# RWKV-7 with a hard-swish FFN on one core: turns of b and k from TensorE to VectorE, copies of y to GpSimd, scan ends to ScalarE

## The chip, the cores and the metric

The kernel runs on one core of one Trainium2 chip. The time is the device time of one execution in microseconds. Before the change three runs took 773.76, 773.98 and 776.44 us, median 773.98 us.

## What is computed

An attention block of the RWKV-7 kind feeds an FFN. For each of 4 batches and 8 heads (head dimension 40) a 40x40 state goes through 768 time steps:

```python
y[:, :, t] = np.einsum('bhd,bhde->bhe', rt, state)
Sa = np.einsum('bhde,bhe->bhd', state, at)
state_decay = state * wt[:, :, None, :] - np.einsum('bhd,bhe->bhde', Sa, bt)
state = state_decay + np.einsum('bhd,bhe->bhde', vt, kt)
```

y, as 3072 tokens of 320 features, is x of the FFN: `h = x @ w_in` (2048 wide), `g = h * clip(h + 3, 0, 6) / 6`, `out = g @ w_out`. The two weights come as 64-bit floats and are made into 32-bit ones on the chip.

## The kernel before

**Units.** The recurrence is computed in blocks of 64 time steps. A unit is one such block of a pair of batches: 128 partitions hold two batches of 64 steps, or, once turned, two heads of 64 (40 used) features. There are 24 units, i = 0 to 23; four make a group. For every unit `prepare(i)` (L582) makes what does not depend on the state, and `step(i)` (L883) what does:

- W, gam: w is turned by TensorE (L506), ScalarE writes it into `wm` (L595, L599), two scans on VectorE (L603, L614) give the cumulative products. gamma (`gam`) and its inverse (`rgam`) are put together from the ends of both scans: two copies of the second scan's result (L626 on ScalarE for the first four units, L628 on VectorE after them) and two by GpSimd (L632, L633).
- A, B, K: a, b and k turned so that features are on the partitions, times gamma or its inverse (L650, L658, L736). From unit 8 on a is not turned by TensorE: it is loaded "by quarters" (L478: 32 partitions for 32 time-step pairs, so that a transpose of 32x32 blocks on VectorE, L528, does the turn). b is turned by TensorE in eight halves (L516) from unit 8 on, k in four whole turns (L506); both products read PSUM.
- F, E, factor, EV: products of these (L672 or L685, L554, L752), the inverse's turn (L705) and K and B times the inverse on GpSimd (L725), which read the untransposed b and k.
- R, C, S, U, UT, rS, H, ysn in `step`: products with the state; ysn (L1064) gives y and the new state. r is loaded by quarters too and turned by VectorE (L531).
- move, move2: y goes into `xt`, the FFN's input, with features on the partitions: four DMAs for the first 256 features (L1111) and four of 32 partitions for the last 64 (L1116). `xt` has six rotating buffers, shared with two partial sums.

For each group the matrix 1 - F of all its units is inverted on VectorE in a chain of some 60 small operations with transposes at both ends (`invert`, L784 to L818), fed in between other work.

**FFN.** `expand` (L1171, L1184, L1193, L1194) and `contract` (L1219) work in pieces of four matmuls, handed out one by one between the attention's stages (`pieces`). An expand needs the two buffers of h, which are free once VectorE has made gt of the one before (L1194).

**Order.** The order of all instructions on each engine is that of the program text. From unit 4 on `a_block(m)` emits step m; a unit takes four steps. Stages of the unit at hand and of units ahead are emitted together: products first, in the order of PRODUCTS (L1463), then the rest in the order of RESULTS (L1465). Unit u >= 8 begins to be prepared at step max(3(u - 8), 4(u - 9)): 0, 3, 6, 9, 12, 16, 20 and so on; so the first four follow one another in three steps, the rest in four.

**Queues.** Nearly all DMAs are issued by SyncE, in program order; a load waits in that queue until its buffer is free, and what is behind it waits too. A unit has 2 loads of w, 4 of a, 2 of b, 2 of k, 8 of r, 4 of v, 8 moves and 2 stores of the output.

**Weights.** 20 pieces; pieces of the first 256 features are loaded by two DMAs, of 80 and 48 partitions (FEATURES, L259).

Of the kernel before, what the change touches and what calls it, by code (L numbers as in the profile page):

```python
# [17 lines left out]
P = 128  # L18
BL = 64
# [12 lines left out]
def kernel(  # L32
# [179 lines left out]
    area = const.tile([P, EDGE + 3 * H * BL], F32, name="area")  # L212
# [30 lines left out]
    tinv = const.tile([P, NH, BL], F32, name="tinv")  # L243


    state, last_dec = [], []
    for p in range(NP):
# [12 lines left out]
        [(0, 0, 2 * D), (2 * D, 4 * D, D + 8)],  # L260
        [(0, 2 * D, 2 * D), (2 * D, 6 * D, D + 8)],
        [(0, 5 * D + 8, L), (L, 7 * D + 8, L)],
# [188 lines left out]
    def fetch(name, i, engine=None):  # L451

        if i is None or i >= NK:
            return
        x, crossed = {"W": (w, 0), "A": (a, 0), "B": (b, 0), "K": (k, 0), "R": (r, 1),
                      "V": (v, 1)}[name]
        if name == "V":
            t = values[i % AHEAD]
        else:
            t = placed.get((name, i))  # L460
            if (name, i) == ("R", 1):
                t = others["K"]
            if (name, i) == ("W", NU + 1):
                t = values[NU]
            t = t if t is not None else (others if i < 2 * NU and i % 2 and name != "R" else inputs)[name]
        g, p = names[i]
        engines = engine or nc.sync
        if name == "R" and i >= NU or name == "A" and i >= 2 * NU:
            y = x[2 * p:2 * p + 2, :, g * BL:(g + 1) * BL, :]
            n = 2 if name == "R" else 1  # L470
            y = y.rearrange("q (k s j) t e -> s j (q k) (t e)", s=2, j=n).rearrange(
                "s j k (l e) -> s j l k e", e=2 * D)
            for s in range(2):
                for c in range(0, D, L):
                    z = s * SLOT + c
                    to = rooms[name][z:z + L].rearrange("l (j k e) -> l j k e", j=n, e=2 * D)
                    for j in range(n):
                        nc.sync.dma_start(out=to[:, j, :, 0:2 * D - c], in_=y[s, j, :, :, c:])  # L478
            data[i][name + "N"] = t
            return  # L480
# [43 lines left out]
    def turn_blocks(to, name):  # L524

        x = rooms[name].rearrange("p (j k y e) -> p j k y e", j=2, y=2, e=D)[:, :, :, :, 0:L]
        if name == "A":
            nc.vector.transpose(out=to[:].rearrange("p r (q t y) -> p q r y t", q=2, y=2), in_=x)  # L528
            return
# [32 lines left out]
    def begun_beside():  # L562

        begin = -(-(SCAN + 1) // 16) * 16
        for n, name in enumerate("KB"):
            x = area[:, begin + n * H * JOIN:begin + (n + 1) * H * JOIN]
            nc.gpsimd.memset(x, 0.0)
            beside[name] = x.rearrange("p (h t) -> p h t", h=H)
        beside["E"] = grp.tile([P, H, BL], F32, name="E", tag="U", bufs=1)
        nc.gpsimd.memset(beside["E"][:], 0.0)  # L570
        for name in "rgam", "RT":
            beside[name] = tmp.tile([P, NPR, P], F32, name=name, tag="rgam", bufs=2)
# [9 lines left out]
    def prepare(i, F):  # L582
        n, o = i % NU, data[i]
        halves = i >= 2 * NU
# [23 lines left out]
        def gam_stage():  # L608
# [15 lines left out]
            def copy(to, x):  # L624
                if i < NU:
                    nc.scalar.activation(out=to, in_=x, func=AF.Copy)  # L626
                else:
                    nc.vector.tensor_scalar(to, x, 1.0, None, ALU.mult)  # L628

            copy(gv[:, :, 0:HB], _ap(o["wm"], HB + 1, [[row, NB], [-1, HB]]))  # L630
            copy(rv[:, :, HB:BL], _ap(o["wm"], HB + 3, [[row, NB], [1, HB]]))
# [6 lines left out]
            if NU + 1 < i <= 2 * NU:  # L638
                fetch("V", i)
            yield from ()  # L640
# [12 lines left out]
        def b_stage():  # L653
            x = turn_in(o["BN"], halves)
            yield PE
            bt = o["bt"] = turned("bt")
            for y, z, g in zip(parts_of(bt, halves), x, parts_of(o["rg"], halves)):
# [74 lines left out]
        def k_stage():  # L732
            x = turn_pairs(o["KN"])
            yield PE
            kt = o["kt"] = turned("kt")
            nc.vector.tensor_tensor(out=kt[:], in0=x[:], in1=o["rg"][:], op=ALU.mult)  # L736
# [24 lines left out]
        return {"W": w_stage, "gam": gam_stage, "A": a_stage, "B": b_stage, "F": f_by_32 if i < 2 * NU else f_by_64,  # L761
# [121 lines left out]
    def step(i):  # L883
# [216 lines left out]
        def s_move():  # L1100
            xt = m["xt"] = ffn.tile([P, 3, P], F32, name="xt", bufs=6)
            yg = m["yg"]
            moves = m["moves"] = [(xt[0:D, 0:2], yg[0:D, 0:2, :]),
                     (xt[D:2 * D, 0:2], yg[SLOT:SLOT + D, 0:2, :]),
                     (xt[2 * D:3 * D, 0:2], yg[0:D, 2:4, :]),
                     (xt[3 * D:P, 0:2], yg[SLOT:SLOT + 8, 2:4, :])]
            for c in range(4):
                moves.append((xt[c * L:(c + 1) * L, 2],
                              yg[SLOT + 8:SLOT + D, 2 + c % 2, :]))
            for dst, src in moves[:4]:  # L1110
# [3 lines left out]
        def s_move2():  # L1114
            for dst, src in m["moves"][4:]:
                nc.sync.dma_start(out=dst, in_=src)  # L1116
# [94 lines left out]
    def contract(i, r, gts):  # L1211
# [13 lines left out]
        if r == 0:  # L1225
            sums[i] = op
            if split:
                part = ffn.tile([P, 3 * P], F32, name="part", tag="xt", bufs=6)[:, 0:DM]
# [219 lines left out]
    for _ in range(18):  # L1448
# [10 lines left out]
    AHEAD_STAGES = [["W", "gam"], ["A", "B"], ["F", "K"], ["E", "factor"], ["EV"]]  # L1459
    CLOSE_STAGES = [["W", "gam"], ["A", "B"], ["F", "K", "factor"], ["E"], ["EV"]]  # L1460
# [4 lines left out]
    RESULTS = ["ysn", "W", "VT", "EV", "R", "S", "C", "A", "B", "move", "move2", "open",  # L1465
               "U", "UT", "rS", "F", "K", "fade", "H", "E", "factor", "RT", "gam"]
# [42 lines left out]
    def a_block(m):  # L1509

        if coming and begins[coming[0]] == m:
            u = coming.popleft()
            close = coming and begins[coming[0]] < m + BLOCKS
            ahead[u, m] = prepared(u), CLOSE_STAGES if close else AHEAD_STAGES
# [29 lines left out]
    for i in range(NU, NK):  # L1544
        spread[0] = i >= 2 * NU - 1
        for j in range(BLOCKS):
# [20 lines left out]
            m += 1  # L1567
    for _ in range(2):
# [36 lines left out]
```

## Time and profile before

| | |
|---|---|
| runs | 773.76, 773.98, 776.44 us |
| profiled execution, its own time | 772.7 us |
| its span | 771.0 us |
| mean granted TensorE clock | 0.956 |
| DMA | 48.43 MB in 175999 packets, 159216 of them under 512 B |
| DMA share in the span's 40 slices, first to eighth | 9, 6, 8, 5, 5, 6, 3, 4 tenths |
| TensorE busy, 300 to 760 us | 20.00 of every 20 us |
| VectorE busy, 500 to 520 us (an inversion) | 18.80 of 20 us |
| VectorE busy, 540 to 560 us | 9.14 of 20 us |

Rows of groups read: line, engine, operation, written tile <- read tiles, shapes and count | busy time in us, mean ns of one | idle time of the engine just before them, and what ended it. In the chain and in timelines each row is a start and a length in us, then what ran; SPq is SyncE's queue, whose length is the time that it took to issue the DMAs (a wait that a DMA instruction itself holds is part of it).

### The profile page before, as it was taken

What the parts mean: (1) busy time and instruction counts of PE and PEld (TensorE: products, weight loads), DVE (VectorE), ACT (ScalarE), POOL (GpSimd) and SP (SyncE); (2) the same over time, 40 slices, a digit from 0 to 9 for tenths busy, and PEclk for the clock granted to TensorE, in tenths of its full rate; (3) what the DMA queues carried; (4) which work ended last, traced back from release to release, by engine and by line L of the source; (5) the groups of instructions that cost most, each with busy time, mean ns of one, the idle gap of its engine ahead of it and who ended that gap; (6) DMA issues with size and microseconds to landing.
All of it is one profiled execution on the core that took longest, in us unless ns stands there. A gap on an engine that the chain in (4) does not pass through costs nothing.

```text
span 771.0 us, 33034 instructions
## 1 busy us (share of the span) xinstructions
PE 710.8 (92%) x14568; PEld 603.1 (78%) x14568; DVE 508.8 (66%) x1027; ACT 310.4 (40%) x644; POOL 150.8 (20%) x303
## 2 busy tenths in 40 slices
PE   4635888999899989999999999999999999999997
PEld 3534777778779778888888888888888888888885
DVE  8899968588557799556798456898436982333210
ACT  2377865232553324552434453234444224322211
POOL 7403210321322211212112121203112010000000
PEclk7956799999999999999999999999999999999999
DMA  9685563420334322233322223313331110110000
GB/s 124 119 179 150 114 170 57 79 43 18 64 65 84 70 55 48 52 71 60 64 52 55 53 62 63 69 37 60 57 72 42 25 24 23 35 35 12 14 16 19
DMA packets 175999, 48.43 MB, mean 63 GB/s; under 512 B 159216, under 2 KB 174576, under 8 KB 175856
## 3 DMA queue, kind: packets, MB, share of 16 engines
q1 hardware_dynamic: 171552, 45.58, 29.7%
q8 instruction: 115, 1.88, 1.0%
q10 hardware_dynamic: 4304, 0.74, 0.7%
q14 instruction: 28, 0.23, 0.1%
HBM read 37.62 MB, written 3.93 MB: 54 GB/s over the span
## 4 chain that ended last, share of the span: by engine, by line
PE 77%; DVE 8%; SPq 5%; issue 3%; DMA 3%; ACT 3%; POOL 0%; DVEq 0%; ACTq 0%; POOLq 0%
PE o L1219 25%; PE h L1171 24%; PE pair L554 4%; PE pair L1064 4%; SPq L490 3%; PE h L1184 2%; PE one L506 2%; PE pair L968 2%; PE pair L927 1%; DVE prod L804 1%; PE pair L1007 1%; PE pair L516 1%; PE pair L752 1%; DVE x L810 1%; PE pair L1023 1%
## 5 line engine op out<-in xcount | busy, mean ns | idle before, releaser
L1171 PE MATMUL h<-xt,win 128*128 128x128 f32 (+1 forms) x2000 | 229.2, 282 | 3.0 <-DVE gt L1194 3.0
L1219 PE MATMUL o<-wout,gt 128*128 128x320 f32 x768 | 230.4, 443 | 0.0
L1171 PEld LDWEIGHTS h<-xt,win 128*128 128x128 f32 (+1 forms) x2000 | 212.9, 193 | 17.5 <-issue 3.1
L1219 PEld LDWEIGHTS o<-wout,gt 128*128 128x128 f32 x768 | 138.6, 190 | 50.3 <-issue 0.2
L1193 ACT ACTIVATE gt<-h,three 128x512 f32<-128x512 f32 x96 | 62.6, 686 | 110.3 <-PE h L1171 88.0
L1194 DVE SCALAR_TENSOR_TENSOR gt<-gt,h 128x512 f32<-128x512 f32 x96 | 61.8, 679 | 62.4 <-ACT gt L1193 62.3
L578 DVE COPY_PREDICATED area<-mask,pair 128x512 f32<-128x512 int32 x56 | 40.5, 726 | 55.2 <-PE pair L554 36.7
L804 DVE TENSOR_TENSOR prod<-x 128x30 f32<-128x30 f32 (+9 forms) x180 | 64.1, 356 | 8.9 <-POOL x L789 3.3
L810 DVE TENSOR_TENSOR x<-x,prod 128x30 f32<-128x30 f32 (+9 forms) x180 | 63.0, 350 | 5.5
L725 POOL TENSOR_TENSOR KBt<-K,rgt 128x320 f32<-128x320 f32 x22 | 19.1, 866 | 142.2 <-ACT rgt L714 134.2
L1071 DVE TENSOR_TENSOR ys<-pair,ys 128x512 f32<-128x512 f32 x20 | 13.8, 690 | 40.5 <-PE pair L1064 40.5
L993 POOL COPY area<-V 128x320 f32<-128x320 f32 x20 | 9.1, 454 | 149.6 <-DVE area L645 53.7
L757 ACT ACTIVATE EV<-pair 64x320 f32<-64x320 f32 x44 | 19.0, 432 | 39.2 <-PE pair L752 38.9
L1064 PE MATMUL pair<-area,KBt 64*64 64x104 f32 x1280 | 32.4, 250 | 0.0
L1237 ACT ACTIVATE ob<-o 128x320 f32<-128x320 f32 x22 | 9.6, 435 | 56.6 <-PE o L1219 35.2
L603 DVE TENSOR_TENSOR_SCAN prods<-area,start 128x528 f32<-128x528 f32 x24 | 29.9, 1250 | 3.4 <-ACT area L599 3.3
L632 POOL COPY gam<-prods 128x256 f32<-128x256 f32 x24 | 12.7, 531 | 99.1 <-DVE prods L603 99.1
L614 DVE TENSOR_TENSOR_SCAN area<-area,start 128x528 f32<-128x528 f32 x24 | 30.6, 1276 | 0.8
L1064 PEld LDWEIGHTS pair<-area,KBt 64*64 64x64 f32 x1280 | 29.9, 133 | 1.5 <-issue 1.4
L872 ACT ACTIVATE tinv<-pair 32x256 f32<-32x256 f32 x48 | 18.0, 375 | 31.9 <-PE pair L862 31.3
L931 DVE TENSOR_TENSOR RR<-pair,EV 128x320 f32<-128x320 f32 x22 | 10.7, 485 | 20.9 <-PE pair L554 13.6
L633 POOL COPY rgam<-prods 128x256 f32<-128x256 f32 x22 | 23.9, 1084 | 0.0
(289 smaller groups left out, 1078.5 us busy)
## 6 DMA issues: line engine op xcount, KB each, us to landing
V<-in_v_dram SPq DMA_DIRECT2D x96, 40.0 KB
out_dram<-ob SPq DMA_DIRECT2D x47, 80.0 KB
R<-in_r_dram SPq DMA_DIRECT2D x92, 40.0 KB
B<-in_b_dram SPq DMA_DIRECT2D x42, 80.0 KB
K<-in_k_dram SPq DMA_DIRECT2D x42, 80.0 KB
W<-in_w_dram SPq DMA_DIRECT2D x37, 80.0 KB
A<-in_a_dram SPq DMA_DIRECT2D x37, 80.0 KB
xt<-yg SPq DMA_DIRECT2D x72, 40.0 KB
```

Source lines behind the costliest of these rows:

```text
L554: nc.tensor.matmul(out=o[i][half(q), n ^ (2 * q * placed), :], lhsT=lhs[half(i, D), n ^ (2 * q * swap), half(q)], rhs=rhs[half(i, D), n, h ...
L578: nc.vector.copy_predicated(out=x[:].rearrange("p (i h) t -> p i h t", i=2), mask=mask8, data=o[2])
L603: nc.vector.tensor_tensor_scan(out=prods[:].rearrange("p r m i -> p (r m i)"), data0=wm[:, 0:SCAN], data1=start[:], initial=0.0, op0=ALU.m ...
L614: nc.vector.tensor_tensor_scan(out=back, data0=back, data1=start[:], initial=0.0, op0=ALU.mult, op1=ALU.add)
L633: nc.gpsimd.tensor_copy(rv[:, :, 0:HB], o["prods"][:, :, 0, 0:HB][:, :, ::-1])
L804: nc.vector.tensor_tensor(out=pv, in0=_ap(x[:], (i + 1) * L + i, [[L, n], [0, i]]), in1=_ap(x[:], i * L, [[0, n], [1, i]]), op=ALU.mult,)
L810: nc.vector.tensor_tensor(out=rest, in0=rest, in1=pv, op=ALU.add)
L1064: nc.tensor.matmul(out=both[q][half(s), pr, :], lhsT=o[name][half(q), h * D:h * D + SLOT], rhs=beside[name][half(q), 4 * rs + 2 * (s ^ (q ...
L1171: nc.tensor.matmul(out=hp[c][:, i, :], lhsT=lhsT, rhs=rhs, start=(begun[c] == 0), stop=(begun[c] == 3 * NQ - 1))
L1193: nc.scalar.activation(out=gt[:], in_=hp[c][:], func=AF.Relu, bias=three[:], scale=1.0)
L1194: nc.vector.scalar_tensor_tensor(out=gt[:], in0=gt[:], scalar=6.0, in1=hp[c][:], op0=ALU.min, op1=ALU.mult)
L1219: nc.tensor.matmul(out=op[:], lhsT=gts[c][:, n, :], rhs=wout[:, c * HJ + r * NQ + n, :], start=((split or r == 0) and c == 0 and n == 0), ...
```

## The change

1. For units 9 and later b and k are loaded a second time, by quarters (names Bq and Kq, four DMAs each), and turned by VectorE into the tiles bt and kt, which are then multiplied in place by the inverse of gamma. TensorE's turns of b and k go. The loads in the old form stay, for GpSimd's products (L725). The stages are called Bq and Kq in the order lists, stand where B and K stood among RESULTS, and are no PRODUCTS.
2. Rooms: Bq lies at the end of `area`, which is cleared by one more GpSimd memset when unit 4 begins; Kq lies in two of the six `xt` buffers, which become one tile `xts`; the FFN's input rotates over four, the two partial sums have the other two, until Kq takes them at step 2.
3. The ends of the second scan are copied in a stage "edge" of their own. For units 8 and later it stands a step after gam, and ScalarE makes the copies; units 4 to 7 keep VectorE.
4. Features are laid out anew so that the last 64 are the first 32 of their heads; for units 4 and later the four moves of these (move2) are GpSimd copies instead of DMAs. The weights' pieces of the first 256 features are now 80, 40 and 8 partitions.

```diff
     FEATURES = [
-        [(0, 0, 2 * D), (2 * D, 4 * D, D + 8)],
-        [(0, 2 * D, 2 * D), (2 * D, 6 * D, D + 8)],
-        [(0, 5 * D + 8, L), (L, 7 * D + 8, L)],
+        [(0, 0, 2 * D), (2 * D, 4 * D, D), (3 * D, 5 * D + L, D - L)],
+        [(0, 2 * D, 2 * D), (2 * D, 6 * D, D), (3 * D, 7 * D + L, D - L)],
+        [(0, 5 * D, L), (L, 7 * D, L)],
     ]
...
+        rooms["Bq"] = area[:, TAIL:]
+        nc.gpsimd.memset(rooms["Bq"], 0.0)
+        fetch("Bq", 2 * NU + 1)
...
-            copy(gv[:, :, 0:HB], _ap(o["wm"], HB + 1, [[row, NB], [-1, HB]]))
-            copy(rv[:, :, HB:BL], _ap(o["wm"], HB + 3, [[row, NB], [1, HB]]))
+            o["edges"] = [(gv[:, :, 0:HB], _ap(o["wm"], HB + 1, [[row, NB], [-1, HB]])),
+                          (rv[:, :, HB:BL], _ap(o["wm"], HB + 3, [[row, NB], [1, HB]]))]
+            if not halves:
+                yield from edge_stage()
...
+        def edge_stage():
+
+            for to, x in o["edges"]:
+                if i < NU or halves:
+                    nc.scalar.activation(out=to, in_=x, func=AF.Copy)
+                else:
+                    nc.vector.tensor_scalar(to, x, 1.0, None, ALU.mult)
+            yield from ()
...
         def b_stage():
-            x = turn_in(o["BN"], halves)
+            x = [None] if by_quarters else turn_in(o["BN"], halves)
             yield PE
             bt = o["bt"] = turned("bt")
+            if by_quarters:
+                x = parts_of(bt, halves)
+                turn_blocks(bt, "Bq")
+                fetch("Bq", following(i))
...
         def k_stage():
-            x = turn_pairs(o["KN"])
+            x = None if by_quarters else turn_pairs(o["KN"])
             yield PE
             kt = o["kt"] = turned("kt")
+            if by_quarters:
+                x = kt
+                turn_blocks(kt, "Kq")
+                fetch("Kq", following(i))
...
-            xt = m["xt"] = ffn.tile([P, 3, P], F32, name="xt", bufs=6)
+            xt = m["xt"] = xts[:, i % NU].rearrange("p (c t) -> p c t", t=P)
...
         def s_move2():
-            for dst, src in m["moves"][4:]:
-                nc.sync.dma_start(out=dst, in_=src)
+            for c in range(4):
+                dst, src = m["xt"][c * L:(c + 1) * L, 2], m["yg"][SLOT:SLOT + L, 2 + c % 2]
+                if i < NU:
+                    nc.sync.dma_start(out=dst, in_=src)
+                else:
+                    nc.gpsimd.tensor_copy(dst, src)
...
-    AHEAD_STAGES = [["W", "gam"], ["A", "B"], ["F", "K"], ["E", "factor"], ["EV"]]
+    AHEAD_STAGES = [["W", "gam"], ["edge", "A", "B"], ["F", "K"], ["E", "factor"], ["EV"]]
...
-    RESULTS = ["ysn", "W", "VT", "EV", "R", "S", "C", "A", "B", "move", "move2", "open",
-               "U", "UT", "rS", "F", "K", "fade", "H", "E", "factor", "RT", "gam"]
+    RESULTS = ["edge", "ysn", "W", "VT", "EV", "R", "S", "C", "A", "B", "Bq", "move", "move2", "open",
+               "U", "UT", "rS", "F", "K", "Kq", "fade", "H", "E", "factor", "RT", "gam"]
...
+            if m == 2:
+                assert not any(x in sums for x in range(SPLIT))
+                rooms["Kq"] = _ap(xts[:], (XT - SPLIT) * 3 * P, [[1, 2 * H * D]])
+                nc.gpsimd.memset(rooms["Kq"], 0.0)
+                fetch("Kq", 2 * NU + 1)
```

## The prediction

> **What bounds the kernel now.** I read the page first, for the span, the busy shares and the chain that ended last:
>
> ```profile
> span 771.0 us, 33034 instructions
> PE 710.8 (92%) x14568; PEld 603.1 (78%) x14568; DVE 508.8 (66%) x1027; ACT 310.4 (40%) x644; POOL 150.8 (20%) x303
> PE 77%; DVE 8%; SPq 5%; issue 3%; DMA 3%; ACT 3%; POOL 0%; DVEq 0%; ACTq 0%; POOLq 0%
> ```
>
> TensorE carries the chain, but SPq, SyncE's issuing of DMAs, has 5%. Next, the chain cut to one group of four units, 317 to 428 us: all of its pieces are TensorE's, so there a microsecond less on TensorE is a microsecond off the end. The turns that the change removes stand in it:
>
> ```profile
> 358.39 0.44 PE one L949 x4
> 358.82 0.39 PE pair L516 x8
> 359.21 0.61 PE pair L927 x32
> ...
> 363.74 0.44 PE one L506 x4
> 364.17 0.60 PE pair L968 x32
> ```
>
> L516 here is b (8 half turns), L506 is k (4 full ones). From 205 to 757 us the waits of TensorE add up to 4 us, three of them at 271 to 281 us behind VectorE. Last, SyncE's own timeline. Between 195 and 273 us it issues one DMA after the other without a pause:
>
> ```profile
> 221.42 3.14 SPq L1111 DMA_DIRECT2D xt<-yg  x4
> 224.61 3.20 SPq L1116 DMA_DIRECT2D xt<-yg  x4
> 227.85 2.67 SPq L487 DMA_DIRECT2D V<-in_v_dram  x4
> ...
> 241.71 2.75 SPq L478 DMA_DIRECT2D A<-in_a_dram  x4
> 244.50 2.99 SPq L487 DMA_DIRECT2D V<-in_v_dram  x4
> ...
> 256.69 2.16 SPq L490 DMA_DIRECT2D W<-in_w_dram  x2
> ```
>
> The second column is the time SyncE spends on issuing. Four quarter loads of a (L478) take 2.03, 1.92, 2.75 and 2.05 us there, 2.2 with the gap between groups. The first products that read those two V loads are
>
> ```profile
> 235.54 0.68 PE L752 MATMUL pair<-V,E 64*64 64x40 f32 x32
> 252.58 0.68 PE L752 MATMUL pair<-V,E 64*64 64x40 f32 x32
> ```
>
> **TensorE's part.** Units 9 to 23 lose both turns. b costs 0.39 us where it follows the turn of the state, and 0.34 with 0.08 of a change of tile shape where a short FFN part stands before it (six such parts become sixteen 64x64 products, 0.92 instead of 1.00 us). k costs 0.44. 15 x (0.39 + 0.44) = **-12.5 us**. Bounds: 0.24 (L516 behind another half turn) to 0.42 for b, 0.44 to 0.59 (L506 at 239.98) for k: 10.2 to 15.2.
>
> **VectorE's part.** Each of these units gains two transposes and loses two copies:
>
> ```profile
> L528 DVE STREAM_TRANSPOSE at<-A 128x512 f32<-128x512 f32 x16 | 11.0, 689 | 0.0
> L628 DVE TENSOR_SCALAR gam<-area 128x256 f32<-128x256 f32 x20 | 5.6, 281 | 1.2
> ```
>
> +2 x 0.69 - 0.28 - 0.30 = +0.8 us of 27.8 in a unit where VectorE is two thirds busy. What hides it is slack: before kt's product E at least 3.9 us, before F behind bt 1.3 us where it is least (366 and 477 us). bt comes 0.69 later and F 0.83 earlier, but VectorE's queue there also starts 0.57 earlier by the missing copies and 0.39 earlier by b's turn, so F waits some 0.2 us or not at all. In the inversions (380 to 420, 500 to 520 us) VectorE is over 90% busy and the FFN's gt comes 1.4 us ahead of its need at 402; it falls 1.6 us behind TensorE there. I put **+0.4** for these; without that cover each would cost up to 0.69. The copies that leave VectorE sit between the scan and gt, and at 271 to 281 us TensorE waits for just that order: **-0.6**. bt and kt are now made from two operands in SBUF. The row beside: a product of 128x58 took 0.53 us at 483.44, under a GpSimd select of 0.51 us, and its neighbour 0.22. The Trainium skill (SBUF — State Buffer, "SBUF: two separate sides") has a lock for this: a VectorE operation with two SBUF inputs and a GpSimd operation that reads SBUF exclude each other. By it F's 0.2 us could be 0.5 more in a few units.
>
> **ScalarE and GpSimd.** 32 copies of 0.42 us (L626's mean) are 13.4 us more on ScalarE, 40% busy. They stand first in their step, the scan is long done, and the product with gamma is behind the transpose of a; nothing, unless a relu stands ahead of them: 0 to 2 us in all. GpSimd's copies of 32x128 are not in the trace: 0.33 (128x16, L635) to 0.53 us (128x256, L632), I take 0.4, nearest in bytes moved in a partition to the second. Four in 20 units are 32 us on an engine 20% busy; behind them wait gamma's copies, which wait for the scan anyway, and the FFN's short product a step later: nothing, at worst 2 us. New memsets: b's room, 640 wide, 0.65 us by L567's 0.79 for 832, on the chain at 194 us (GpSimd, then scale, then VectorE): +0.65, against 0.57 for the copies just behind: **+0.1**.
>
> **SyncE's part.** Per unit 8 quarter loads come, 2 x 2.2 = 4.4 us, and four moves (L1116, 2.5 to 3.2 us) go. Up to the first V above there are four groups more (Bq and Kq of units 9 and 10) and one group of moves less, and SyncE starts 0.4 earlier because it is idle until 195.2: 4 x 2.24 - 3.25 - 0.4 = 5.3 us later. V's last issue starts at 235.2 instead of 229.9. A quarter load issued at 264.40 landed 1.76 us later, so V is there at 237.0. By then TensorE is 3 turns ahead, 1.2 us, and wants it at 234.3: a stall of 2.7 us. Two groups more stand before the second V: 9.8 us late, there at 258.3. TensorE wants it at 252.58 - 1.2 + 2.7 - 0.83 = 253.2: a stall of 5.1. W of unit 12 (256.69) then comes 7.3 us late, there at 267.5, wanted at 267.3: 0.2. From 273 SyncE waits 7.8 us for VectorE and catches up. Later it has 20 us of waiting in a group of 111.6 and gets 7 us more work; V is 4.3 us or more ahead and loses 2.9 in a unit. **+8.0 us**; bounds 0 (the loads land earlier than I reckon) and 12.
>
> **The weights' loads.** Four pieces before 55 us and four after it are split 80/40/8 instead of 80/48, one DMA more for each. The chain at the start:
>
> ```profile
> 38.66 0.42 SPq L343
> 39.12 5.73 DMA raw<-in_moe_w_in_dram
> ```
>
> Four more issues of 0.47 us ahead of the third load on the chain (52.10) are 1.9, and two at 80 to 86 us, ahead of moves on the chain at 95, up to 0.9. **+2.0**, bounds 0 (DMA, not the issue, is late) and 4.5.
>
> **Sum.** -12.5 + 0.4 - 0.6 + 0.1 + 8.0 + 2.0 = -2.6 us. The profiled execution took 772.7 us with a span of 771.0; it would take 770.1. The runs shown have a median of 773.98, 1.3 above; from that the forecast is **771.4**. About 0.5%, 3.9 us, is what a measurement of this kernel can tell from no change.
>
> **Rivals.**
> *The loads arrive in time.* SyncE's group times hold pauses of some 0.9 us that need not grow with the number of DMAs, and V may land sooner. For it: TensorE waits for no load after 205 us now. Against: no pause in SyncE between 195 and 273. Without the 8.0: 763.4.
> *SyncE becomes the bound for good, slower.* In three of four units of a group SyncE now waits 2.2 to 4.5 us. If the new loads cost as in the crowded stretch (2.75), a unit gets 3 us more and TensorE takes 0.8 less, and once V's lead of 4.3 us is used up each of some nine units to 600 us loses about 1 us: 771.4 + 9 = 780.4. It decides from 4.3 us of lasting lateness. Against it: the fourth unit of each group waits 10 us, which clears the queue.
> *The weights land later.* With 80 and 48 rows all DMA engines carry alike; if 40 and 8 rows use fewer, the fullest carries ten rows instead of eight of a piece, and the 5.73 and 4.09 us on the chain grow by a quarter, 2.4 us: 773.8. The Trainium skill (DMA: Bandwidth & Descriptors, "Why a DMA increments its semaphore by 16 and not by 1") says so: a DMA runs on the largest number up to 16 that divides its slowest dimension, here 10 and 8. The page of before shows no such split.
> *It doesn't free TensorE.* If what follows the removed turns waits for the new ones on VectorE (F behind bt, gt in the inversions), a third of the gain goes: 4 us: 775.4.
>
> **Chances.** Forecast 0.45 (its own range 768 to 775; 0.09 of it under 770.1), loads in time 0.27, SyncE the bound 0.14, weights 0.07, TensorE not freed 0.07. Faster by over 0.5% (under 770.1): 0.27 + 0.09 = 0.36. Slower by over 0.5% (over 777.9): 0.14 and 0.02 of the last, 0.16. Within: 0.48. The range goes from the full gain, 763.0, to 778.5 and leaves out most of the slow case and the lower end of the fast one.
>
> **What would show it.** Right: V's loads at some 233 and 254 us on SyncE, waits of TensorE before L752's line there of 3 and 5 us, no other wait over 1 us after 205, units 27.0 instead of 27.8 us apart after 320. Wrong: no wait there (fast case); waits for V or W after 320 (slow case); the third load's landing at 55.4 as now, or 4 us later; F waiting for bt, h for gt. Most at risk is the rate at which SyncE issues.

## The result: slower by half a per cent

The changed kernel took **777.64 us** (median of 20 runs, 773.32 to 782.61) against 773.87 us of the kernel before (median of 20, 771.90 to 779.99): a ratio of 1.0046, 95% interval 1.0029 to 1.0062. By the medians it lost 3.8 us, where 2.6 us less were forecast. The profiled execution took 782.34 us, 4.7 above its own median, with a span of 780.6 us; so its trace shows the loss in a large form.

These lines of the changed kernel's page answer to the prediction's first lines, of the kernel before:

```profile
span 780.6 us, 32997 instructions
PE 708.2 (91%) x14484; PEld 598.0 (77%) x14484; DVE 523.9 (67%) x1025; ACT 320.1 (41%) x676; POOL 175.9 (23%) x385
...
PE 59%; DVE 18%; issue 6%; SPq 6%; DMA 4%; ACT 4%; POOL 1%; DVEq 0%; POOLq 0%; ACTq 0%
```

TensorE's share of the chain fell from 77 to 59%, and VectorE's rose from 8 to 18%.

To see where the time went, I set the traces side by side by one product that each of the last 20 units has once, that of the state beside the scores (L1064 before, L1083 after). It starts first at 214.0 us before and 216.3 after; at the fourth unit it stands at 303.7 and 319.9; at the last at 726.7 and 737.1. So the changed execution is 2.3 us late at the first, loses **13.9 us** up to the fourth, and gains 5.8 us from there. The two largest groups of TensorE's waits at 205 to 330 us (total, times, longest):

```profile
PE h L1191 <- DMA xts<-yg: 7.0, 2, 4.2
PE pair L771 <- DMA V<-in_v_dram: 3.6, 3, 2.3
```

The first line is two waits for the FFN's input moves (xts<-yg), of 2.9 us up to 235.4 and 4.2 us up to 304.2; between them stand the three waits for V, at 259 to 263. In the kernel before the waits in this stretch add up to 4.0 us, none of them for a DMA. SyncE's timeline there (start, time spent issuing):

```profile
228.16 2.84 SPq L482 DMA_DIRECT2D area<-in_b_dram  x4
231.04 3.15 SPq L1127 DMA_DIRECT2D xts<-yg  x4
...
236.19 3.63 SPq L491 DMA_DIRECT2D V<-in_v_dram  x4
...
258.75 2.59 SPq L491 DMA_DIRECT2D V<-in_v_dram  x4
...
294.79 3.04 SPq L482 DMA_DIRECT2D A<-in_a_dram  x4
...
299.85 3.08 SPq L1127 DMA_DIRECT2D xts<-yg  x4
```

The moves (xts<-yg) stand in line behind the quarter loads (area<-in_b is b's room, xts<-in_k k's). At 231 us the line itself doesn't wait: SyncE issues without a pause from 196.7 to 289.2 us, and the moves, at 221.4 us before, come 9.6 us later. At 300 us it does wait: the load of a may start only when VectorE has emptied its room, SyncE stands still from 289.2 to 294.8 for that, and the moves are behind it, 17.0 us later than before (282.9). The same places by windows (stretch, its length, PE busy, granted clock, the DMA engines' share, GB/s):

```profile
232.00:236.00 4.00, 1.12 (x34) 0.80 0.22 59
236.00:240.00 4.00, 4.00 (x52) 0.50 0.34 66
...
300.00:304.00 4.00, 0.08 (x1) 0.83 0.25 65
304.00:308.00 4.00, 3.77 (x18) 0.50 0.09 22
```

Behind the two waits for moves, and behind those for V too (0.50 at 264 to 268 us), the granted clock is half, while TensorE works for 5.8, 9.3 and 5.2 us; before, all these rows have 1.00. The DMA engines are mostly idle in these rows, and the moves are not slow on the way: the last of the four took 1.8 us from the start of its issue to its landing, before (223.9 to 225.7 us) and after (233.5 to 235.4). They are late in the queue. The Trainium skill ("TensorE: Matmul & The Clock Gate", Part 1: the HAM clock gate) has this: an idle stretch of about 3.4 us halves the clock, and as long a busy one gives it back. The trace agrees in kind, not in the number: the clock fell 1.8 us into the wait of 2.9 us (at 234.37 us), and at 261.68 us, behind a wait for V of 2.3 us and in the midst of the next; more on this at the end.

### The profile page after: what moved, and what is told of

Same layout as the page of the kernel before. It is cut to its first block, busy times and chain, and to the rows that moved or that the text cites. A ratio compares the mean times of both kernels' runs of the same rounds, so it can differ in the third digit from the quotient of the medians.

```text
span 780.6 us, 32997 instructions
## 1 busy us (share of the span) xinstructions
PE 708.2 (91%) x14484; PEld 598.0 (77%) x14484; DVE 523.9 (67%) x1025; ACT 320.1 (41%) x676; POOL 175.9 (23%) x385
## 4 chain that ended last, share of the span: by engine, by line
PE 59%; DVE 18%; issue 6%; SPq 6%; DMA 4%; ACT 4%; POOL 1%; DVEq 0%; POOLq 0%; ACTq 0%
PE h L1191 19%; PE o L1239 19%; PE pair L558 3%; PE pair L1083 3%; DVE prod L823 3%; DVE x L829 3%; PE h L1204 2%; DVE area L620 2%; SPq L494 2%; SPq L1127 1%; DVE gt L1214 1%; DVE prods L609 1%; PE pair L987 1%; SPq L482 1%; PE pair L946 1%
## 5 line engine op out<-in xcount | busy, mean ns | idle before, releaser
L1191 PE MATMUL h<-xts,win 128*128 128x128 f32 (+1 forms) x1904 | 225.7, 285 | 11.0 <-DMA xts<-yg 7.0
L1239 PE MATMUL o<-wout,gt 128*128 128x320 f32 x768 | 233.5, 448 | 0.0
L1191 PEld LDWEIGHTS h<-xts,win 128*128 128x128 f32 (+1 forms) x1904 | 210.5, 195 | 24.5 <-DVE x L829 4.6
L1136 POOL COPY xts<-yg 32x128 f32<-32x128 f32 x80 | 43.2, 540 | 155.1 <-DVE yg L1093 147.9
L1083 PE MATMUL pair<-area,KBt 64*64 64x104 f32 x1280 | 32.4, 250 | 0.0
L1083 PEld LDWEIGHTS pair<-area,KBt 64*64 64x64 f32 x1280 | 29.9, 133 | 1.5 <-issue 1.4
L891 ACT ACTIVATE tinv<-pair 32x256 f32<-32x256 f32 x48 | 18.0, 374 | 23.6 <-PE pair L881 23.0
L1204 PE MATMUL h<-xts,win 64*64 64x128 f32 x800 | 27.6, 275 | 0.0
L957 ACT ACTIVATE VT<-pair 128x512 f32<-128x512 f32 x22 | 13.1, 597 | 31.2 <-PE pair L558 19.4
L845 POOL COPY tinv<-tb 32x1024 f32<-32x1024 f32 x10 | 10.3, 1034 | 63.0 <-DVE tb L832 56.2
```

Of the source, the lines that this page charges most:

```text
L1083: nc.tensor.matmul(out=both[q][half(s), pr, :], lhsT=o[name][half(q), h * D:h * D + SLOT], rhs=beside[name][half(q), 4 * rs + 2 * (s ^ (q ...
L1136: nc.gpsimd.tensor_copy(dst, src)
L1191: nc.tensor.matmul(out=hp[c][:, i, :], lhsT=lhsT, rhs=rhs, start=(begun[c] == 0), stop=(begun[c] == 3 * NQ - 1))
L1204: nc.tensor.matmul(out=hp[c][half(z), i, :], lhsT=y[:, half(z)], rhs=xt[half(c), 2, :], start=(begun[c] == 0), stop=(begun[c] == 3 * NQ - 1))
L1239: nc.tensor.matmul(out=op[:], lhsT=gts[c][:, n, :], rhs=wout[:, c * HJ + r * NQ + n, :], start=((split or r == 0) and c == 0 and n == 0), ...
```

## Experiments

**The theory** was: the turns leave TensorE as forecast, but SyncE's time for issuing the quarter loads holds up what stands behind them, V and the FFN's moves, between 214 and 304 us; each wait costs again by the clock. **Rivals:** VectorE, by its new turns, is what is late; or the other parts (split weights, GpSimd's copies, ScalarE's edges) cost the time; later also that the transfers, not their issuing, are late.

All ratios are to the kernel before, measured again beside each run. The last three columns are from one trace each, against the trace of before by the product above: the lateness at the first unit (214 us), what is added up to the fourth (304 us), and from there to the last. The first of these differs by some us between executions of kernels that are alike up to there (2.3 in the changed kernel's trace, 7.9 in e3's), so the middle column is the one to read. Of an edit in several places the line that matters is shown.

| kernel | us | ratio, 95% | at 214 | to 304 | to the last |
|---|---|---|---|---|---|
| changed | 777.64 | 1.0046 (1.0029 to 1.0062) | +2.3 | +13.9 | -5.8 |
| e1 quarter loads left out | 768.89 | 0.9923 (0.9891 to 0.9954) | +2.0 | -0.8 | -6.6 |
| e2 no quarters | 775.30 | 1.0002 (0.9978 to 1.0027) | +3.0 | -0.4 | +1.6 |
| e3 from unit 13 | 774.66 | 0.9985 (0.9961 to 1.0009) | +7.9 | -1.4 | -3.3 |
| e4 quarters on ScalarE | 819.11 | 1.0568 (1.0532 to 1.0604) | +8.7 | +10.1 | +31.3 |
| e5 moves first | 777.80 | 1.0028 (1.0006 to 1.0051) | +4.9 | +6.8 | -5.7 |
| e6 waits filled | 780.99 | 1.0073 (1.0048 to 1.0099) | +2.9 | +11.5 | -4.0 |
| e7 old moves | 791.02 | 1.0199 (1.0168 to 1.0231) | -0.5 | +10.8 | +4.9 |
| e8 from unit 11 | 774.87 | 0.9992 (0.9967 to 1.0017) | +2.0 | 0.0 | -0.3 |
| e9 small quarters | 771.16 | 0.9942 (0.9917 to 0.9968) | +2.2 | +0.5 | -4.8 |
| e10 quarters on GpSimd | 786.41 | 1.0146 (1.0118 to 1.0174) | +9.5 | +2.1 | +2.1 |
| e11 small weights on ScalarE | 780.14 | 1.0063 (1.0034 to 1.0092) | +3.9 | +12.1 | -5.0 |
| e12 e3 with small weights | 773.53 | 0.9990 (0.9971 to 1.0009) | +8.1 | +1.0 | -4.1 |
| e13 k only | 773.68 | 0.9993 (0.9976 to 1.0010) | +2.6 | -0.1 | -0.7 |
| e14 b only | 776.31 | 1.0014 (0.9983 to 1.0045) | +2.7 | +2.4 | -1.5 |
| e15 stores on ScalarE | 782.63 | 1.0113 (1.0089 to 1.0138) | +7.8 | +7.2 | -4.1 |
| e16 k only, stores | 780.02 | 1.0085 (1.0054 to 1.0117) | +8.2 | +3.7 | -0.7 |
| e17 k from unit 13, old moves | **771.70** | **0.9961 (0.9943 to 0.9979)** | +0.5 | -0.1 | -0.3 |
| e18 from unit 13, old moves | 782.08 | 1.0111 (1.0093 to 1.0130) | -0.1 | +4.4 | +5.8 |

**e1, the loads left out.** What SyncE does for the quarters of units 10 to 23 goes, the turns stay (of unit 9's b and k, which stay in their rooms).

```
-        if i is None or i >= NK:
+        if i is None or i >= NK or name[1:] and i > 2 * NU + 1:
```

> Leaves out the quarter loads of b and k of units 10 to 23: unit 9's stay in the rooms and are turned again and again, so later outputs are made from unit 9's b and k. All of VectorE's, GpSimd's, ScalarE's and TensorE's work of the change stays; SyncE issues 8 loads a unit less and no longer waits for VectorE's turns of b and k. Theory (SyncE's queue: between 214 and 320 us the FFN's input moves and V stand behind quarter loads, TensorE waits for them in three places, 13 us, and the granted clock is 0.5 for some 8 us behind each wait): these waits go, unit 9's state product at 320 us in the changed kernel starts near 303, and the whole takes 763 to 767. Rival VectorE (the turns make VectorE late, and the moves are late because of it): the waits stay, 774 to 778. Rival of the other parts (GpSimd's copies, ScalarE's edges, the split weights): 775 to 778.

768.89 us: 1.9 above the theory's range, and far from both rivals. Of the 13.9 us nothing is left. The waits of TensorE at 205 to 330 us:

```profile
PE h L1191 <- DVE gt L1214: 4.4, 3, 2.4
...
PE h L1191 <- DMA xts<-yg: 0.2, 1, 0.2
```

None for V, 0.2 us for moves. But 4.4 us for gt, VectorE's part of the FFN, have come up, at 287 and 301 us above all, in the inversion. All waits in this stretch are 6.4 us where the kernel before has 4.0, which accounts for a gain of 0.8 up to 304 us in place of the four units' 3.3. The VectorE rival has a true share here, which the later moves of the changed kernel would hide.

**e2, no quarters** (turns on TensorE as before, the other parts kept).

```
-        halves, by_quarters = i >= 2 * NU, i > 2 * NU
+        halves, by_quarters = i >= 2 * NU, False
```

> Undoes the turns: b and k are turned by TensorE as before, no quarter loads. GpSimd's copies for the last 64 features, ScalarE's edges a block later and the split weights' loads stay. Theory (SyncE's queue): the start costs 2.3 us at 214 us, SyncE has four DMAs a unit less than before and no wait of TensorE over 1 us follows, VectorE loses 0.57 us of copies a unit: 774 to 776. Rival of the other parts: they cost the time by themselves, 777 to 780. If they are a gain that the quarters eat up: under 772.

775.30 us, no difference from before: by the interval the other parts cost at most 2.1 us, about what the start loses, and do not make the loss.

**e3, from unit 13 on.**

```
-        halves, by_quarters = i >= 2 * NU, i > 2 * NU
+        halves, by_quarters = i >= 2 * NU, i >= 13
```

> Turns by VectorE from quarter loads only from unit 13 on (11 units in place of 15); units 9 to 12, whose loads fall in the crowded stretch, are turned by TensorE as before. Theory (SyncE's queue): nothing is lost between 214 and 320 us, the four units' turns (3.3 us) come back, and the rest gains 0.6 to 0.83 us a unit: 773.9 + 2.3 - (6.6 to 9.1) = 767 to 770. Rival VectorE: the first units that are turned by VectorE lose their time wherever they stand: waits of 3 us and more at 330 to 420 us, 774 to 778. Rival of the other parts: 775 to 778 too, but with the loss before 320 us.

Nothing lost up to 304 us and 3.3 us gained after it, with no wait for a move or V. But 774.66 us, not under 770: the gain is half of the least that I reckoned for 11 units, and this trace was 7.9 us late at the first unit. The time lies in the rival VectorE's range; its sign, waits of 3 us at 330 to 420 us, is missing (one of 0.8 us, for no engine).

**e4, the quarter loads from ScalarE's queue.**

```
-                        nc.sync.dma_start(
+                        (nc.scalar if name[1:] else nc.sync).dma_start(
```

> Issues the quarter loads of b and k from ScalarE's queue in place of SyncE's. SyncE then has less work a unit than before the change; ScalarE has 8 issues of some 0.45 us a unit more and waits in order for VectorE's turns. Theory (SyncE's queue): TensorE no longer waits for moves or V between 214 and 320 us: 763 to 768 if ScalarE's copies are not held up, 768 to 774 where they are. Rival VectorE: 775 to 779, the waits for moves stay. Rival of the other parts: 775 to 779.

819.11 us, worse than any theory said. SyncE is relieved, but the load of the next unit waits for VectorE's turn of this one, and now ScalarE's copies stand behind that. The group that lost most on ScalarE (after the bar: busy time, mean ns, then the idle time ahead of it and what ended it):

```profile
L891 ACT ACTIVATE tinv<-pair 32x256 f32<-32x256 f32 x48 | 18.0, 375 | 50.9 <-DMA area<-in_b_dram 25.5 <-PE pair L881 10.3 <-DVE kt L532 9.4
```

50.9 us of idle time, where this group has 23.6 in the changed kernel, nearly all behind TensorE. A queue that waits is cheap only on an engine that has nothing else to do.

**e5, the moves ahead of the loads** (one place, that of the wait at 300 us).

```
-"A", "B", "Bq", "move", "move2", "open",
+"move", "move2", "open", "A", "B", "Bq",
```

> The changed kernel with one difference in order: the FFN's input moves stand ahead of the loads of a and b where they are put out in one block, which is so at one place, that of the 4.2 us wait at 300 us. Theory (SyncE's queue holds the moves up behind loads that wait for VectorE's turns, and the clock is at half behind the wait): the wait at 300 us goes and with it the cold stretch at 304 to 312; the waits at 232 and 259 us stay: 5 to 7 us less than the changed kernel, 771 to 773. Rival (TensorE would wait there for VectorE anyway, for gt or bt): under 2 us less, 776 to 778.

A ratio of 1.0028 against 1.0046, whose intervals overlap: no gain that can be told. In the trace the wait at 300 us is gone, and in its place:

```profile
PE h L1191 <- DVE gt L1214: 4.6, 3, 2.5
PE h L1191 <- DMA xts<-yg: 2.9, 1, 2.9
```

The second line is the wait at 236 us, which this edit doesn't touch; the first stands at the inversion and was 0.6. So the rival of this run was right: TensorE waits there for gt anyway. Its stretch to 304 us is 7 us better than the changed kernel's, but the changed kernel's trace is 4.7 us above its own median.

**e6, the waits filled with products.** This tests the clock: TensorE works where it waited, with 5 products ahead of unit 4's first h and 7 ahead of unit 6's.

```
+        for _ in range(idle):
+            nc.tensor.matmul(out=hp[0][:].rearrange("p n t -> p (n t)")[:, 0:DM], lhsT=win[:, 0, 0:P],
+                             rhs=wout[:, 0, :], start=True, stop=True)
```

> Adds work: 5 and 7 products of 128x320 (0.57 us each, 2.9 and 4.0 us) on constants on TensorE just where it waits 2.9 us at 232 us and 4.2 us at 300 us for the FFN's input; what they write is overwritten. Theory (each such wait costs again as much by the clock granted after it, 0.5 for some 8 us): the waits are filled, the clock stays at 1.0 at 236 to 242 and 304 to 311, and the time falls by about 3.4 us for each: 770 to 774. Rival (the clock falls for another reason, or the wait alone counts): no gain, 777 to 782.

The clock did what I said, the time did not: 780.99 us, in the rival's range. The windows of this run:

```profile
236.00:240.00 4.00, 3.51 (x60) 1.00 0.46 86
240.00:244.00 4.00, 3.44 (x69) 1.00 0.59 97
```

TensorE keeps its full clock here, and at 304 to 312 us too, and then waits at 241 us for V (3.44 of 4.00), which it had not done in the changed kernel. V is issued at 237.3 and 257.6 us, where it was 236.2 and 258.8: **SyncE sets the pace in this stretch**, and TensorE's slow six microseconds only take time from its next wait. So at the first wait the clock is a sign of the loss and not a term of its own. At the third it was worth something: this trace gained 1.5 us on the changed kernel's up to 320 us, and lost as much in the next unit, with a stop of 1.6 us at 332 (of the kind told of at the end). For the waits for V, which stayed, nothing is shown. In the time no gain is left of it, and this part of my theory fell.

**e7, the old layout of moves and weights** (four moves a unit back on SyncE).

```
-                nc.gpsimd.tensor_copy(dst, src)
+                nc.sync.dma_start(out=dst, in_=src)
```

> Quarters and ScalarE's edges as in the changed kernel, but the features are laid out as before: the weights' pieces are split in two, and the last 64 features go by four moves on SyncE instead of GpSimd's copies. Theory (SyncE's queue): each of units 4 to 6 has 3.2 us more of SyncE in the crowded stretch, the waits there grow by 3 to 6 us and their cold stretches with them; the start gets 2.3 us back: 779 to 786. Rival (the split weights and GpSimd's copies are what costs): 770 to 775.

791.02 us, even more than the theory's range. The first unit is on time (-0.5), which puts the late start on the split weights. After 330 us SyncE is too full again and again, and TensorE waits for V, six times:

```profile
PE pair L771 <- DMA V<-in_v_dram: 6.1, 6, 2.6
```

**e8, from unit 11 on**, with the order of e5 and the first loads issued by unit 10's stages.

```
-        fetch("Bq", 2 * NU + 1)
...
-                fetch("Bq", following(i))
+            if i >= 10:
+                fetch("Bq", following(i))
```

> Turns by VectorE from quarter loads from unit 11 on (13 units), the first quarter loads issued by unit 10's stages, and the FFN's input moves ahead of the loads as in the run with moves first. Theory (SyncE's queue): some eight groups of quarter loads less than in the changed kernel stand in SyncE's stretch from 196 to 262 us, no wait for a move or V of over 1 us is left, and 13 units gain 0.57 us each (b's turn 0.37 and k's 0.53 less 0.32 that the FFN's pieces beside them get longer, as the changed kernel's trace shows after 440 us), against 2.3 us at the start: 768 to 771. Rival VectorE (its turns make bt, kt and gt late in the inversions): 774 to 778.

0.8 us are left of the waits for V and none for moves, as expected, but the time is 774.87 us, that of the kernel before and in the rival's range: 3.8 us of waits for gt have come in. At this place its chain shows VectorE slowed down as well:

```profile
296.95 0.36 DVE x L830
...
297.33 0.89 DVE prod L824
...
298.25 0.89 DVE x L830
```

Two operations on shrinking tiles took 0.89 us where their neighbour took 0.36, while GpSimd ran two products of 1.07 and 0.96 us (KBt, from 296.95; the kernel before has them too). It fits the lock of the Trainium skill (SBUF — State Buffer, "SBUF: two separate sides") that the prediction named; the price here was 1.1 us.

**e9, small quarter loads** (as many DMAs, an eighth of the bytes).

```
-    nc.sync.dma_start(out=to[:, j, :, 0:2 * D - c], in_=y[s, j, :, :, c:])
+    few = slice(0, 4 if name[1:] else L)
+    nc.sync.dma_start(out=to[few, j, :, 0:2 * D - c], in_=y[s, j, few, :, c:])
```

> The changed kernel with the same number of quarter loads in the same places, but each moves 4 of its 32 partitions, an eighth of the bytes and packets; the rest of the rooms keeps what was there, so what is computed from b and k is not the reference's. Theory (what counts is the time that SyncE spends on issuing, and the waits at the head of its queue): TensorE still waits at 232, 259 and 300 us, and the time is that of the changed kernel within 3 us, 775 to 780, unless the issues themselves become shorter. Rival (the packets of the quarter loads fill the DMA engines and make moves and V land late): as in the run with the loads left out, 767 to 771.

771.16 us, at the upper end of the rival's range. The theory's own reservation holds too, for the issues did become shorter:

```profile
226.00 1.69 SPq L483 DMA_DIRECT2D area<-in_b_dram  x4
227.73 3.16 SPq L1128 DMA_DIRECT2D xts<-yg  x4
...
232.49 3.31 SPq L492 DMA_DIRECT2D V<-in_v_dram  x4
```

A group takes 1.3 to 1.7 us, median 0.30 a DMA, where the full ones take 1.8 to 3.2, median 0.45. That alone takes the moves and V from 231.0 and 236.2 to 227.7 and 232.5 us, and the wait for moves at 232 us is gone. One of 2.4 us stays at 289 to 291 us; the profile puts it down to VectorE's inversion, but the moves were issued there from 286.9 to 289.9 us, again behind a load that waited for VectorE's turn. Waits for V of 1.6 us in all are left. Since bytes and issue time fell together, this run by itself does not tell issuing from transfer. Two things in the changed kernel's trace do: the DMA engines are 37 to 47% busy in stretches of 20 us at 200 to 300 us, and neither the moves (1.8 us, as before) nor V took longer to land than before (the last of four 2.2 and 2.3 us from the start of its issue, 3.1 and 2.6 before).

**e10, the quarter loads from GpSimd's queue.**

```
+                        (nc.gpsimd if name[1:] else nc.sync).dma_start(
```

> Issues the quarter loads from GpSimd's queue in place of SyncE's. SyncE then has four DMAs a unit less than before the change. Theory (SyncE's queue): the waits for moves and V at 232 and 259 us go. What it costs on GpSimd is not seen in any trace here: if an issue takes no longer there than on SyncE (0.45 to 0.6 us, some 4 us of the 20 us a unit that GpSimd has idle) 768 to 772, and if GpSimd's copies and the product KBt are held up by it, as ScalarE's were in its run, 785 to 820. Rival VectorE: 775 to 779 with the waits for moves still there.

TensorE waits for no move and no V any more, which bears the theory out; VectorE's gt makes it wait instead, 7.0 us up to 330 us and 5.0 later, and the time is 786.41 us, at the low end of the bad case. (Its start is the latest of all, 9.5 us.) GpSimd's row for one of the two loads:

```profile
L482 POOL DMA_DIRECT2D area<-in_b_dram x60 | 35.1, 591 | 70.2 <-DVE bt L532 68.7 <-issue 1.2 <-POOL area L575 0.3
```

0.59 us an issue, and 68.7 us in which GpSimd stood waiting for bt's turn, with gamma's copies behind it.

**e11 and e12, the small weights' pieces from ScalarE's queue**, in the changed kernel and with e3.

```
-                nc.sync.dma_start(out=to, in_=src)
+                (nc.scalar if to.shape[0] == D - L and issued[0] <= 4 else nc.sync).dma_start(out=to, in_=src)
```

> The changed kernel, but the four pieces of 8 rows that the split weights add to the first four loads are issued from ScalarE's queue. Theory of the start (the split costs 2 to 2.5 us by SyncE's issues ahead of the third load on the chain, 1.3 us of it before 41 us): half of it comes back, 1 to 2 us less than the changed kernel, 775.5 to 777; the first state product at 215.0 to 215.5 us instead of 216.3. Rival (the start is late by the transfers, not by the issues): no change, 777 to 778.5.

> Turns by VectorE from unit 13 on, and the 8-row pieces of the first four weights' loads issued from ScalarE's queue: the two together. If the start's cost is in SyncE's issues: 1 to 2 us less than the run from unit 13 on, 772.5 to 774, and 1 to 2.5 us below the kernel before. If it is in the transfers: 774 to 775.

780.14 and 773.53 us: the start does not get better (+3.9 and +8.1 at 214 us), so four issues less on SyncE do not bring it back; nor do the ratios fall (1.0063 against 1.0046, 0.9990 against e3's 0.9985). e11 is above both of its ranges; e12 lies where its theory had it, but e3's interval holds it too.

**e13 and e14, one of the turns alone** (e13 shown; e14 has `"B"`, and each leaves out the other's turn and fetch).

```
-    [[x + "q" if x in "BK" and u > 2 * NU else x for x in y] for y in order]
+    [[x + "q" if x == "K" and u > 2 * NU else x for x in y] for y in order]
```

> Only k is turned by VectorE from quarter loads (units 9 to 23); b is turned by TensorE as before. All else as changed. Theory (SyncE's time for issuing, 2.3 us a group of four): half of the lateness in the crowded stretch, so the moves are there when TensorE wants them at 232 us (a wait of 1 us at most) and V at 259 us, against a gain of some 0.35 us a unit (0.53 less the longer FFN pieces): 771 to 774. Rival (VectorE's turns make the waits): half of the changed kernel's loss, 775 to 777.

> Only b is turned by VectorE from quarter loads; k is turned by TensorE as before. Theory (SyncE's issuing): the same half of the lateness, a gain of some 0.2 us a unit (0.37 less the longer FFN pieces): 773 to 775.5. Rival (one of the two is what hurts: F waits for bt): 776 to 779, with waits of F for bt.

773.68 and 776.31 us. With half of the loads the loss up to 304 us is -0.1 and +2.4 us, not half of 13.9: it does not grow in step with the loads. With b alone one wait of 4.0 us for moves is left, with k alone none. e14's time lies in its rival's range, but the rival's sign is missing: F waits 0.3 us for bt. Neither turn makes the loss by itself.

**e15 and e16, the stores from ScalarE's queue**, in the changed kernel and with k alone.

```
-                queue = nc.scalar if q and i == NK - 1 else nc.sync
+                queue = nc.scalar
```

> The changed kernel with the stores of the output issued from ScalarE's queue, behind the copy that makes them ready there; SyncE issues two DMAs, 1.2 us, less a unit. Theory (SyncE's issuing): the moves at 231 us are issued 1.2 us earlier and V at 259 us 2.4 us earlier, and the waits for them shrink by that: 773 to 776. Rival (SyncE's issuing is not what sets these waits): 777 to 779.

> k alone by quarters and the stores on ScalarE's queue: SyncE has 2.3 - 1.2 - 3.2 us a unit against the kernel before, so less than that. Theory (SyncE's issuing): no wait of TensorE for a move or V is left, the gain of k stays: 769 to 773, under the kernel before. Rival (ScalarE is held up by the stores, or k's turn costs VectorE what TensorE gains): 774 to 777.

782.63 and 780.02 us, both missed. Up to 304 us e15 loses 7.2 instead of 13.9, so SyncE's 1.2 us a unit seem to tell, but the first unit is already 7.8 and 8.2 us late. A part of that is ScalarE's: it issues stores ahead of its copies of tinv, and TensorE waits 1.6 and 1.7 us for these at 207 us, which it does not in the changed kernel. The rest may be the spread of the start.

**e17 and e18, the old layout, from unit 13 on**, with k alone and with both.

> Only k by quarters, from unit 13 on; the weights' pieces and the last features' moves as before the change (two pieces, four moves on SyncE a unit). Theory (the start's 2.3 us belong to the split weights, the loss at 214 to 304 us to SyncE's issuing there, the gain to the turns removed): nothing at the start, nothing lost at 214 to 304 us, some 0.35 us a unit gained over 10 units if SyncE, which waits 2.2 to 4.5 us in most units there, has room for 2.3 us more: 770 to 773. If it has not, waits for V as in the run with old moves: 775 to 780.

> b and k by quarters from unit 13 on, weights and moves as before the change. Theory: no loss at the start nor at 214 to 304 us; 4.6 us of quarter loads a unit on SyncE beside the four moves is more than the 2.2 to 4.5 us that it waits, so V is late again at the units behind 440 us as in the run with old moves: 773 to 778. If SyncE's spare time at each group's fourth unit is enough: 768 to 771.

e17 combines the edits of e7, e13 and e3 and is **faster than both kernels**: 771.70 us, 0.9961 (0.9943 to 0.9979). Up to 330 us TensorE waits for no move and no V; later for no DMA at all. The gain rests on the medians, for the trace stands 0.2 us behind that of before at the last product: it gained 3.5 us from 327 to 605 us, where k's turns are gone, but had lost 2.7 in the unit ahead of these, with a stop of 1.5 us (more on such stops at the end). e18, with b too, missed its ranges: 782.08 us, 3.6 us of waits for b's old loads up to 330 us and 4.9 us for V behind it. Beside the old moves SyncE has room for the quarters of one array, not of two.

## Why the prediction was wrong, point by point

**TensorE, -12.5 us: right in most units, too much in the sum.** From the fourth product to the fifteenth (320 to 615 us) the changed kernel gained 0.3 to 1.1 us in nine of eleven units, 7.2 in all or 0.80 each; forecast were 0.83. In the two units behind an inversion (428 to 454 and 538 to 563 us) it lost 0.6 each instead, which leaves 6.0 us of 9.1. The chain at the second of these:

```profile
537.74 1.79 DVE tb L832
...
539.63 2.00 DVE tt L837
...
542.15 0.41 DVE state L1092
...
542.70 0.74 PE pair L858 x48
```

TensorE, now earlier, waits for VectorE's turns behind the inversion; before, this stretch of the chain is all TensorE's. That is the rival "it doesn't free TensorE", beside the forecast and not in place of it.

**SyncE, +8.0 us: the step that failed.** It failed in what was late more than in how much SyncE issues. The forecast had V at some 233 and 254 us; it came at 236.2 and 258.8, 1.9 us of that because SyncE started at 196.7 and not at 194.8. It landed 2.2 and 2.3 us after the start of its last issue, where 1.76 was reckoned. V was then waited for 3.6 us and not 7.8, since TensorE had already been held up. But I had priced only V and W, and the same queue carries the FFN's input: their moves, 9.6 and 17.0 us late, gave the two largest waits, 7.0 us, which stand nowhere in my sum. Nor does the half clock behind the waits. And "from 273 SyncE waits 7.8 us for VectorE and catches up" was the second half of the error: it issued on until 289.2, and the wait, there 5.6 us, was no pause to catch up in but one with moves behind it. In the profiled execution the stretch costs 13.9 us, where 8.0 less the four units' 3.3 would be 4.7. By the medians the loss in it is smaller: 3.8 us in all, less a start of 2.3 and a gain of 5.8, leaves about 7 us. This is an estimate, and a loose one, since the start lies between 2.0 and 9.5 us in the traces with split weights. By it the miss of 6.4 us has two parts of like size: some 2.5 us here, and 3.3 in the gain after 304 us, 5.8 instead of 9.1.

**The weights, +2.0: right in size, its cause open.** The third load landed at 56.9 us (54.24 and 2.66) instead of 55.35, and the first state product came 2.3 us later; without the split (e7, e17, e18) it came -0.5 to +0.5 us later, in the other sixteen traces 2.0 to 9.5. So the split costs something, and 2.3 is at the low end. What the prediction took from the Trainium skill (DMA: Bandwidth & Descriptors, "Why a DMA increments its semaphore by 16 and not by 1"), that fewer engines carry the pieces, made no load longer: the raw load on the chain took 5.63 us with 40 and 8 rows and 5.73 with 48. That the issues make the lateness was not borne out by e11 and stays open.

**VectorE, +0.4 and -0.6.** Too small: without the loads TensorE waits 4.4 us for gt in the first inversion (e1), though in the changed kernel these hide behind the moves. **ScalarE and GpSimd, nothing:** right as far as e2's interval tells. GpSimd's copies took 0.54 us each, not 0.4:

```profile
L1136 POOL COPY xts<-yg 32x128 f32<-32x128 f32 x80 | 43.2, 540 | 155.1 <-DVE yg L1093 147.9
```

**The rivals.** "SyncE the bound for good" had the right engine and the wrong place: the loss is over at 320 us, and 320 to 737 us is a gain. It came true in e7 and e18, where SyncE has the moves as well. "Loads in time" (763.4) is nearest to e1, which has none to wait for: 768.9, in part because VectorE's gt then makes TensorE wait. **Open:** why the start differs so much between executions, and by what the split weights delay it.

## What to carry to other kernels

Before a transfer is added to a queue, list everything that stands behind it there, with the moment each is needed, and not only the transfers that look alike; and count what the new one waits for itself, since all behind it wait too. A relief of the bounding engine is worth its price only where another has slack: here the same edit was a loss in the crowded 90 us and a gain of 6.0 us in the eleven units after them, so begin it behind the crowd. That alone does not make it pay: e3 did so and cannot be told from the kernel before; e17 also went back to the old layout and left b's turns on TensorE. Moving loads or stores to the queue of an engine that computes (e4, e10, e15) was worse each time; in e4 and e10 that engine then stood waiting with its own work behind.

## What was not expected of the hardware

The granted clock does not go by the length of the last wait alone. In e8, by windows of 2 us, a wait of 2.41 us (300.8 to 303.3) left it at 1.00, and one of 1.52 us (320.7 to 322.2) brought it to half:

```profile
302.00:304.00 2.00, 0.74 (x6) 1.00 0.70 118
304.00:306.00 2.00, 2.00 (x55) 1.00 0.27 46
...
322.00:324.00 2.00, 1.76 (x4) 0.69 0.71 138
324.00:326.00 2.00, 2.00 (x11) 0.50 0.26 44
```

What tells them apart is where they lie. In all twenty traces the records of the granted clock change only whole multiples of 3.41 us apart (here at 322.74 and 326.16). Cut at these places, the time falls into stretches of 3.41 us. Between 150 and 755 us the clock fell to half after 46 of them, and in each of these TensorE was idle for 1.4 us or more; no stretch with over 1.9 us of idle time kept it, and between 1.4 and 1.9 us both happened. It came back only after a stretch in which TensorE was idle for 0.01 us at most. The wait of 2.41 us lies across a border, at 302.26 us, and so counts as 1.41 and 1.00; the one of 1.52 lies inside one stretch.

TensorE's single stops of 0.6 to 1.6 us for which the profile shows no releaser (at 320.7 us in e8, at 332 in e6, at 319 in e17) go with loads of instructions. In the traces other than e4's there are 21 of them between 205 and 757 us, and each ends 1.25 to 1.57 us after the end of a load of 16 KB on the page's queue "instruction", whose loads end some 6 us apart (median). That TensorE ran out of instructions there is inferred from this; no run tests it. If so, an edit can lose 1.5 us in a place that it doesn't touch, as e17 seems to have.

SyncE's time for one DMA depends on what it moves, and not on its bytes alone: a quarter load of 24 to 40 KB took 0.45 us (median), one with an eighth of the packets 0.30, V's loads of 40 KB 0.62 and w's of 80 KB 0.65.
